# Last weights rebuilt from head 29.5 on, own PSUM tile for a chunk's scale sum, two sets of mixes, later sums of squares

## The chip, the cores and the metric

One NeuronCore of a Trainium2 chip runs the whole program. The metric is the device time of one execution in microseconds, lower is better. TensorE (PE) multiplies matrices into PSUM, VectorE (DVE), ScalarE (ACT) and GpSimd (POOL) do the rest, and SyncE (SP) issues most DMAs. Each engine works through its own list of instructions in order.

## The reference

Three stages, float32 in the result:

```python
# attention: B,H,S,D = 4,8,576,64; decay from cumulated log f, causal softmax
scores = scale * q @ k.T + cum[:, :, :, None] - cum[:, :, None, :]
x = softmax(causal(scores)) @ v                      # -> (4, 576, 512)
# moe: gated MLP, d_model 512, d_ff 1024
h = relu(x @ w_in); u, v = h[..., :512], h[..., 512:]
v_s = einsum('ts,bsd->btd', w_spatial, layernorm(v)) + b_spatial[None, :, None]
x = (u * v_s) @ w_out
# moe2: each token mixed with the one before it
xk = mu_k * x + (1 - mu_k) * x_prev
xr = mu_r * x + (1 - mu_r) * x_prev
k = relu(xk @ w_k)
out = sigmoid(xr @ w_r) * (k * k @ w_v)
```

## The kernel before

Most weights and operands arrive as 64-bit numbers or are kept as a high and a low 16-bit half, so that three matmuls (T3) stand for one product of more exact numbers. A weight block of 128x512 is fetched raw by one DMA of 512 KB (`raw_load`), rebuilt as float32 by one ScalarE and three VectorE instructions (`raw_convert`), squared and summed by ScalarE (`sumsq`), scaled and split into halves (`w2_split`: `scalar.mul`, then a subtraction on VectorE).

The order is written as a list of steps with due times in units of a head (32 heads, `add(t, prio, fn, ...)`); `run` sorts them. The program order that comes out is a priority: a planner of the build places each engine's instructions by a simulated time line, and only instructions given to `pin` keep the program order among themselves. So real places differ from the due times.

- Attention runs head by head. The normalisation of a pair of heads passes through small DMAs on SP (`rd`, `r`, `rd`, `sr`; `head`, `recip`), then GpSimd and ScalarE write `xt`.
- The first MLP of batch b (`plan_mlp`: `m1v` with a layernorm `ln1` to `ln4`, `m1u`, `m2`) follows some heads behind. `m2` (L586) ends with the gate on VectorE (L589), the store of `u` to DRAM and the square of `u` on ScalarE (L594, L66). Batch 3's MLP begins at 34.7 and lasts 4.
- `plan_w2` rebuilds 16 blocks: four of w_out at 13.9 and on, eight of w_k at 25.2 and on, four of w_r at 33.6 and on. The first 12 are fetched through ScalarE's queue, the others by SP. `weights2v` rebuilds the eight blocks of w_v into pool p2, which lies where the MLP's pools `acts` and `w` were.
- The last stage runs over five chunks of up to 512 tokens. `m3(i)` multiplies by w_out, stores `x2[i]` and sums its squares; `mix(i, w)` makes the mixed input `xx[w]` (w = 0 for k, 1 for r), after `scale3`, which adds up the squares with a matmul against ones (`total`, L71, name `tot`) and reduces it on VectorE (L836); `chunk(i)` runs m4 (x w_k, relu, square, split into `k2`), m5 (x w_v, accumulated in four PSUM banks), m6 (x w_r, sigmoid) and multiplies into `o` (L919).
- Pieces of `m3(i+2)` and `mix(i+1, w)` are generators that are advanced between the steps of `chunk(i)`.

PSUM has eight banks here: `psm` tag "m" with two, `ps3` tag "p" with four and tag "a" with two. `total` takes its tile from `psm`, and m5's accumulators 0 and 1 lie in `psm`, 2 and 3 in "a":

```python
ps = self.psm.tile([128, 512], F32, tag="m", name="tot")                       # total, L70
q, tag = (self.psm, "m") if j < 2 else (self.ps3, "a")                         # m5
xh = self.xx[w] = p.tile([128, 2, 4, 512], F16, tag=f"xx{w}", bufs=1, ...)      # mix: one set
```

All matmuls that go through the helper `mm` have line L852 in the profile, whatever the stage; they are told apart by their tiles (`xx,w2k` is m4, `w2r,xx` m6, `moe_w_v,k` m5, `g,wstage` m3; `w2r` holds a part of w_k too, so `xx,w2r` is m4).

Of the kernel before, what the change touches and what calls it, by code (L numbers as in the profile page):

```python
# [39 lines left out]
class K:  # L40
# [19 lines left out]
    def split(self, src, hi, lo):  # L60
        self.nc.scalar.copy(hi, src)
        self.nc.vector.tensor_tensor(lo, src, f32(hi), ALU.subtract)
# [510 lines left out]
    def m2(self, b, fc, hf, part):  # L573
# [13 lines left out]
        if part:  # L587
            uu = self.u[:, fc, ts_]
            nc.vector.scalar_tensor_tensor(uu, o, self.sw[:, 3:4], uu, ALU.mult, ALU.mult)  # L589
            if hf:  # L590
                nc.sync.dma_start(self.gd[:, fc, self.S * b:self.S * b + self.S], self.u[:, fc])
                if fc == 0:
                    self.ga[b] = self.c.tile([128, 4], F32, tag="ga", bufs=2, name="ga")
                self.sumsq(self.ga[b][:, fc:fc + 1], self.u[:, fc], self.junka[:, 0:self.S])  # L594

    def plan_mlp(self, b, s, length):
# [15 lines left out]
        add(s + length + 0.3, 3, self.gsum, b)  # L612
# [89 lines left out]
    def w2_last(self):  # L702
# [4 lines left out]
        self.w2["moe2_w_r"] = [w[:, :, k] for k in range(4)]  # L707

    def w2_fetch(self, n, q):
        nm, kc, c = self.blocks[n]  # L710
        self.raw_load(self.raws[n % 2], nm, slice(128 * kc, 128 * kc + 128), slice(c, c + 512), q)

    def w2_conv(self, n):
# [3 lines left out]
        self.sumsq(self.am2[:, n:n + 1], e, self.junka[:, 0:512])  # L717
# [30 lines left out]
    def plan_w2(self):  # L748

        add = self.add  # L750
        add(13.0, 9, self.w2_begin)
# [8 lines left out]
        add(t[3] + 0.7, 7, self.w2_norm, 0)  # L760
        add(t[11] + 0.7, 7, self.w2_norm, 1)
        add(t[15] + 0.7, 7, self.w2_norm, 2)

    def weights2v(self, p):

        nm = "moe2_w_v"
        self.wv = p.tile([128, 2, 8, 512], F32R, name=nm)
        self.raw_load(self.raws[0], nm, slice(0, 128), slice(0, 512), self.nc.sync)
        yield
        for n in range(8):  # L770
            if n < 7:
                self.raw_load(self.raws[(n + 1) % 2], nm, slice(128 * n + 128, 128 * n + 256), slice(0, 512), self.nc.sync)
            e = self.we[n % 3]
            self.raw_convert(self.raws[n % 2], e, True)
            self.split(e, self.wv[:, 0, n], self.wv[:, 1, n])
            yield
# [10 lines left out]
    def phase3(self):  # L787
# [5 lines left out]
        self.g = [t[:, 2048 + 512 * i:2560 + 512 * i] for i in range(2)]  # L793
# [4 lines left out]
    def m3(self, i):  # L798
# [4 lines left out]
        x2 = self.x2[i] = p.tile([128, 4, 513], F32, tag="x2", bufs=3, name="x2")  # L803
# [14 lines left out]
        for kc in range(4):  # L818
            g, s = self.g[kc % 2], gm[:, 2 + kc:3 + kc]
# [12 lines left out]
    def scale3(self, i):  # L832
# [3 lines left out]
        nc.vector.tensor_reduce(sc[:, 0:1], self.total(self.st3[:, 4 * i:4 * i + 4], 4), AX.X, ALU.add)  # L836
# [17 lines left out]
    def mix(self, i, w):  # L854
# [6 lines left out]
        xh = self.xx[w] = p.tile([128, 2, 4, 512], F16, tag=f"xx{w}", bufs=1, name=f"xx{w}")  # L861
# [16 lines left out]
    def chunk(self, i):  # L878
        nc, p = self.nc, self.p3
        sc = self.sc3[:, 8 * i:8 * i + 8]  # L880
        t0, n = self.chunks[i]
        xk = self.xx[0]
# [4 lines left out]
        def m4(fc):  # L887
            ps = self.ps3.tile([128, 512], F32, tag="p", bufs=4, name="m4")
            self.mm(ps[:, 0:n], [(wk[kc][:, ws, 128 * fc:128 * fc + 128], xk[:, s_, kc, 0:n]) for kc in range(4) for s_, ws in T3])
            tmp = p.tile([128, 512], F32, tag="tmp", bufs=3, name="tmp")  # L890
# [17 lines left out]
        xr = self.xx[1]  # L908
# [16 lines left out]
def body(tc, a, out):  # L925
# [39 lines left out]
    wv = k.weights2v(k.p2)  # L965
    for _ in range(3):
        next(wv, 0)
    for x in first:
# [42 lines left out]
```

## Time and profile before

| | |
|---|---|
| time, median of 3 runs | 775.11 us (771.89 to 775.39) |
| time of the profiled run | 772.58 us |
| its span, first to last instruction | 770.8 us |
| mean granted clock of TensorE | 0.962 of full speed |
| TensorE busy | 675.6 us (88%) |
| VectorE, ScalarE, GpSimd busy | 456.6, 412.9, 191.1 us |
| HBM read, written | 42.06, 9.79 MB |

The profile is one execution. Attention ends at about 395 us, the last MLP's m2 at 490, and the chunks' ends are at 536, 606, 673, 733 and 766 us. Busy time of TensorE is modelled, and matmuls overlap a little. In lists of instructions, the text in square brackets is the time that the engine stood idle before the first of them, and whom it waited for.

### The profile page before, as it was taken

Reading aid. Unit: us, or ns where it says so; the run is one execution under the profiler, and the core shown is the slowest. Engines: PE = TensorE matmul, PEld = TensorE weight load, DVE = VectorE, ACT = ScalarE, POOL = GpSimd, SP = SyncE. Lnnn points to the kernel's source line nnn. Section 1 sums busy time; section 2 is a strip of 40 time slices with the busy share of each in tenths; the row PEclk is TensorE's granted clock in tenths of the full one; section 3 lists DMA queues with packets and bytes.
Section 4 is the critical chain, followed back from the end, with each engine's and each line's share of the span. In section 5 each row is a group of like instructions: output and inputs, shape, how many; then the busy total and the mean of one; then the engine's idle time right before and its main releaser. Section 6 shows DMA issues by size and latency. Waiting matters only on the chain.

```text
span 770.8 us, 11313 instructions
## 1 busy us (share of the span) xinstructions
PE 675.6 (88%) x3742; PEld 429.8 (56%) x3742; DVE 456.6 (59%) x1304; ACT 412.9 (54%) x850; POOL 191.1 (25%) x385
## 2 busy tenths in 40 slices
PE   0388977898989989998899989999899799979988
PEld 0245654566765567655665446566355466636565
DVE  5987794668667646677555883484812462192071
ACT  4636884576546653566665893553832353272251
POOL 7123554454435534444332300000000000000000
PEclk9998979999999999999999999999999899999999
DMA  9997867665663424432144311251000100010010
GB/s 228 201 202 159 184 131 155 139 148 115 159 161 102 100 53 76 90 107 70 58 140 144 110 27 45 70 154 57 25 14 1 55 1 1 1 55 0 1 56 27
DMA packets 130683, 69.80 MB, mean 91 GB/s; under 512 B 114704, under 2 KB 115312, under 8 KB 130624
## 3 DMA queue, kind: packets, MB, share of 16 engines
q1 hardware_dynamic: 126304, 61.59, 33.5%
q10 hardware_dynamic: 4320, 7.48, 3.4%
q8 instruction: 29, 0.48, 0.3%
q14 instruction: 30, 0.25, 0.1%
HBM read 42.06 MB, written 9.79 MB: 67 GB/s over the span
## 4 chain that ended last, share of the span: by engine, by line
PE 52%; DMA 16%; DVE 13%; ACT 7%; POOL 5%; issue 4%; SPq 3%; ACTq 0%; DVEq 0%; POOLq 0%
PE m L852 35%; PE o L370 5%; PE m L586 4%; DMA sr<-rd 3%; POOL x L401 3%; DMA rd<-xo 3%; DMA r<-rd 2%; PE m1u L569 2%; PE s L315 2%; DVE junk L324 2%; PE t L348 2%; DMA nat<-in_k_dram 2%; DVE o L919 2%; DMA rd<-r 2%; ACT junka L66 1%
## 5 line engine op out<-in xcount | busy, mean ns | idle before, releaser
L370 PE MATMUL o<-e,v 128*128 128x320 f32 (+4 forms) x448 | 118.0, 395 | 13.6 <-ACT xo L378 7.0
L852 PE MATMUL m<-moe_w_v,k 128*128 128x512 f32 x432 | 110.8, 407 | 0.0
L852 PE MATMUL m<-xx,w2k 128*128 128x512 f16 (+1 forms) x360 | 84.4, 377 | 17.0 <-ACT xx L874 17.0
L370 PEld LDWEIGHTS o<-e,v 128*128 128x128 f32 x448 | 79.8, 204 | 32.7 <-POOL e L357 9.2
L324 DVE CUSTOM_DVE_ANT_0 junk<-s,mask 128x512 bf16<-128x512 f32 (+4 forms) x160 | 75.7, 473 | 28.8 <-PE s L315 23.6
L852 PEld LDWEIGHTS m<-moe_w_v,k 128*128 128x128 f32 x432 | 80.8, 188 | 20.6
L352 ACT ACTIVATE e<-t,qa 128x512 f32<-128x512 f32 (+1 forms) x128 | 71.6, 590 | 33.6 <-PE t L348 31.4
L357 POOL TENSOR_SCALAR_AFFINE_SELECT e<-e 128x128 f32<-128x128 f32 (+1 forms) x160 | 53.2, 351 | 118.3 <-ACT e L352 115.8
L315 PE MATMUL s<-kT,qT 128*128 128x512 f16 (+2 forms) x192 | 55.5, 300 | 24.1 <-DVE nm L324 14.7
L852 PEld LDWEIGHTS <-w2k 128*128 128x128 f16 x360 | 36.2, 103 | 53.5 <-issue 25.0
L893 DVE TENSOR_TENSOR tmp<-tmp 128x512 f32<-128x512 f32 (+1 forms) x40 | 25.1, 638 | 65.7 <-ACT tmp L892 65.5
L401 POOL TENSOR_TENSOR x<-xo,sr 64x576 f32<-64x576 f32 x32 | 47.4, 1481 | 64.5 <-DMA sr<-rd 63.2
L569 PE MATMUL m1u<-xt,win 128*128 128x288 f16 x384 | 55.1, 294 | 5.8 <-ACT u L571 3.5
L348 PE MATMUL t<-qA,kA 69*128 69x512 f16 (+2 forms) x192 | 50.9, 292 | 7.6 <-DMA qA<-md 4.9
L515 PE MATMUL m1v<-win,xt 128*128 128x512 f16 x240 | 57.2, 379 | 0.0
L315 PE MATMUL s<-kA,qA 67*128 67x512 f16 (+2 forms) x192 | 50.6, 302 | 5.3 <-DMA kA<-kT 3.4
L852 PE MATMUL m<-g,wstage 128*128 128x512 f16 (+1 forms) x240 | 54.8, 375 | 0.0
L892 ACT ACTIVATE tmp<-m,w2k 128x512 f32<-128x512 f32 (+1 forms) x40 | 25.1, 644 | 55.0 <-PE m L852 54.9
L586 PE MATMUL m<-wspT,vn 128*128 128x288 f16 x384 | 53.5, 286 | 0.4 <-DVE u L589 0.4
L348 PE MATMUL t<-qT,kT 128*128 128x512 f16 (+2 forms) x192 | 50.2, 292 | 0.0
L569 PEld LDWEIGHTS <-win 128*128 128x128 f16 x384 | 38.3, 101 | 19.7 <-issue 7.4
L852 PE MATMUL m<-w2r,xx 128*128 128x512 f16 x216 | 48.2, 379 | 0.0
(206 smaller groups left out, 1144.1 us busy)
## 6 DMA issues: line engine op xcount, KB each, us to landing
sr<-rd SPq DMA_DIRECT2D x32, 144.0 KB
gd<-u SPq DMA_DIRECT2D x16, 288.0 KB
out_dram<-o SPq DMA_DIRECT2D x18, 256.0 KB
nat<-in_k_dram SPq DMA_DIRECT2D x32, 128.0 KB
v<-in_v_dram SPq DMA_DIRECT2D x32, 128.0 KB
wstage<-in_moe_w_k_dram ACTq DMA_DIRECT2D x8, 512.0 KB
g<-gd SPq DMA_DIRECT2D x16, 256.0 KB
wstage<-in_moe_w_v_dram SPq DMA_DIRECT2D x8, 512.0 KB
```

What stands on the lines that cost most here:

```text
L315: self.nc.tensor.matmul(s[:, o:o + n], self.tok(qn, p, h, 128 * ib - 64, 128)[0:r], self.tok(kn, p, h, k0, n)[0:r], start=(j == 0), stop=( ...
L324: self.nc.vector.tensor_tensor_reduce(out=self.junk[r0:, 0:n], in0=self.s[u % 2][r0:, o:o + n], in1=self.mask[r0:, m0:m0 + n], op0=ALU.add ...
L348: self.nc.tensor.matmul(t[:, o:o + n], self.tok(kn, p, h, 128 * c, 128)[0:r], self.tok(qn, p, h, q0, n)[0:r], start=(j == 0), stop=(j == 1))
L352: self.nc.scalar.activation(self.e[g][:, 512 * u:512 * u + n], t[:, 0:n], AF.Exp, scale=self.qa[p][:, 5:6])
L357: self.nc.gpsimd.affine_select(out=e, in_=e, pattern=[[1, n]], compare_op=ALU.is_ge, fill=0.0, base=0, channel_multiplier=-1)
L370: self.nc.tensor.matmul(o[:, 256 + f:256 + q1], v[:, c, h // 2, 64 * (h % 2):64 * (h % 2) + 128], e[:, off:off + q1 - f], start=(c == 0), ...
L401: self.nc.gpsimd.tensor_tensor(self.xp[r], self.xo[h][r], self.sr[r], ALU.mult)
L515: nc.tensor.matmul(self.m1p, xt[:, xs, 128 * j:128 * j + 128], self.win[:, ws, kc, 512:1024], start=(kc == 0 and n == 0), stop=(kc == 3 an ...
L569: self.nc.tensor.matmul(o, self.win[:, ws, kc, fs], self.xt[(4 * b + kc) % 8][:, xs, ts_], start=(kc == 0 and n == 0), stop=(kc == 3 and n ...
L586: nc.tensor.matmul(o, pairs[n][0], pairs[n][1], start=(n == 0), stop=(n == 13))
L852: self.nc.tensor.matmul(out, l, r, start=(first and j == 0), stop=(last and j == len(pairs) - 1))
L892: nc.scalar.activation(tmp[:, 0:n], ps[:, 0:n], AF.Relu, scale=sc[:, 4:5])
```

## The change

- `total` can take its tile from another pool; `scale3` passes `ps3`, so the chunk's scale sum lies in the ring "p", of four tiles.
- `xx` has two sets: even chunks in p3, odd ones in p2. `k2`, `o` move from p3 to p2; w_v moves from p2 to p3; `x2` has two buffers in place of three; the staging tiles `g` of m3 are three in place of two.
- All 16 blocks of `plan_w2` come from 29.5 on, 0.33 apart, and w_v's eight blocks behind them, 0.36 apart, as steps of the list. All fetches are issued by SP.
- The squares of the weight blocks and of `u` become steps of their own, some tenths of a head later, and are pinned; so is the ScalarE half of w_v's split.
- Before the chunks, `m3(0), m3(1), mix(0, 0), mix(0, 1)` are advanced from the first of the remaining steps on, and all done before the pools are released. In the chunk loop the side work is advanced at each step.

```diff
-    def total(self, col, n):
-        ps = self.psm.tile([128, 512], F32, tag="m", name="tot")
+    def total(self, col, n, p=None):
+        ps = p.tile([128, 512], F32, tag="p", bufs=4, name="tot") if p else self.psm.tile([128, 512], F32, tag="m", name="tot")
...
@@ m2
                 nc.sync.dma_start(self.gd[:, fc, self.S * b:self.S * b + self.S], self.u[:, fc])
-                if fc == 0:
-                    self.ga[b] = self.c.tile([128, 4], F32, tag="ga", bufs=2, name="ga")
-                self.sumsq(self.ga[b][:, fc:fc + 1], self.u[:, fc], self.junka[:, 0:self.S])
@@ plan_mlp
-        add(s + length + 0.3, 3, self.gsum, b)
+            if k == "g" and x[1] and x[2]:
+                add(t + (0.5 if b < 3 else 0.2), 3, self.gsq, b, x[0])
+        add(s + length + (0.7 if b < 3 else 0.3), 3, self.gsum, b)
+    def gsq(self, b, fc):
+        if fc == 0:
+            self.ga[b] = self.c.tile([128, 4], F32, tag="ga", bufs=2, name="ga")
+        self.pin(self.sumsq(self.ga[b][:, fc:fc + 1], self.u[:, fc], self.junka[:, 0:self.S]))
@@ w2_fetch, w2_conv
-        self.raw_load(self.raws[n % 2], nm, slice(128 * kc, 128 * kc + 128), slice(c, c + 512), q)
+        self.raw_load(self.raws[n % 2], nm, slice(128 * kc, 128 * kc + 128), slice(c, c + 512), self.nc.sync)
-        self.sumsq(self.am2[:, n:n + 1], e, self.junka[:, 0:512])
+    def w2_sq(self, n):
+        self.pin(self.sumsq(self.am2[:, n:n + 1], self.e2[n], self.junka[:, 0:512]))
@@ plan_w2
-        t = [13.9 + 1.5 * i for i in range(4)] + [25.2 + 1.0 * i for i in range(8)] + [33.6 + 0.45 * i for i in range(4)]
+        t = [29.5 + 0.33 * i for i in range(16)]
         for n in range(16):
-            add(13.1 if n == 0 else max(24.6 if n == 4 else 0, t[n] - 0.9), 9, self.w2_fetch, n, self.nc.scalar if n < 12 else self.nc.sync)
+            add(29.0 if n < 2 else t[n - 1] + 0.02, 9, self.w2_fetch, n)
             add(t[n], 7, self.w2_conv, n)
             if not 4 <= n < 12 or n % 2:
-                add(t[n] + 0.35, 7, self.w2_split, n)
+                add(t[n] + 0.3, 7, self.w2_split, n)
+            add(t[n] + 0.25, 7, self.w2_sq, n)
...
+        tv = [t[15] + 0.36 * (i + 1) for i in range(8)]
         for n in range(8):
+            add(t[15] + 0.02 if n == 0 else tv[n - 1] + 0.02, 9, self.wv_fetch, n)
+            add(tv[n], 7, self.wv_conv, n)
+            add(tv[n] + 0.25, 7, self.wv_split, n)
@@ phase3, m3
-        self.g = [t[:, 2048 + 512 * i:2560 + 512 * i] for i in range(2)]
+        self.g = [t[:, 2048 + 512 * i:2560 + 512 * i] for i in range(2)] + [self.g2]
-        x2 = self.x2[i] = p.tile([128, 4, 513], F32, tag="x2", bufs=3, name="x2")
+        x2 = self.x2[i] = p.tile([128, 4, 513], F32, tag="x2", bufs=2, name="x2")
@@ scale3, mix, chunk
-        nc.vector.tensor_reduce(sc[:, 0:1], self.total(self.st3[:, 4 * i:4 * i + 4], 4), AX.X, ALU.add)
+        nc.vector.tensor_reduce(sc[:, 0:1], self.total(self.st3[:, 4 * i:4 * i + 4], 4, self.ps3), AX.X, ALU.add)
-        xh = self.xx[w] = p.tile([128, 2, 4, 512], F16, tag=f"xx{w}", bufs=1, name=f"xx{w}")
+        xh = self.xx[i, w] = (self.p2 if i % 2 else p).tile([128, 2, 4, 512], F16, tag=f"xx{w}", bufs=1, name=f"xx{w}")
-        nc, p = self.nc, self.p3
+        nc, p = self.nc, self.p2
@@ body
-    first = (x for y in (k.m3(0), k.mix(0, 0), k.m3(1)) for x in y)
+    first = (x for y in (k.m3(0), k.m3(1), k.mix(0, 0), k.mix(0, 1)) for x in y)
     while k.steps:
         last += 0.25
         k.run(last)
-        if last > G + 2.0:
-            next(first, 0)
+        next(first, 0)
+    for _ in first:
+        pass
...
         for _ in k.chunk(i):
-            next(wv, 0)
-            n += 1
-            if (n <= 5 and i < 3) or n >= 9:
-                next(side, 0)
-            if n == 12:
-                next(side, 0)
+            next(side, 0)
```

## Rows read from the trace of the kernel before

**Rows 1.** Page, engines' busy time, share of the span, instructions.

```profile
PE 675.6 (88%) x3742; PEld 429.8 (56%) x3742; DVE 456.6 (59%) x1304; ACT 412.9 (54%) x850; POOL 191.1 (25%) x385
```

**Rows 2.** Waits of PE from 520 on: us in total, times, longest.

```profile
PE m L852 <- ACT xx L874: 17.0, 4, 4.7
```

**Rows 3.** Timeline of PE around the second boundary: start, us, what.

```profile
608.51 0.28 PE L71 MATMUL tot<-w2k,ones 128*128 128x4 f32 x2
613.45 1.86 PE L852 MATMUL m<-xx,w2k 128*128 128x512 f16 x4 [4.66 <-ACT xx L874]
```

**Rows 4.** Chain of waits over the second boundary: start, us, what.

```profile
606.67 0.66 DVE o L919
...
609.45 0.09 DVE w2k L836
...
610.71 1.96 ACT tmp L871 x3
```

**Rows 5.** Windows behind the boundaries, and the middle of a chunk; PEclk is granted clock.

```profile
core 0: us, PE busy (x) PEld busy (x) DVE busy (x) ACT busy (x) POOL busy (x), PEclk, DMA share, GB/s
543.00:547.00 4.00, 4.00 (x11) 1.46 (x11) 4.00 (x9) 3.73 (x6) 0.00 (x0) 0.57 0.00 0
613.45:617.50 4.05, 4.05 (x16) 2.21 (x16) 4.05 (x10) 3.58 (x6) 0.00 (x0) 0.50 0.00 0
679.50:683.50 4.00, 4.00 (x11) 1.46 (x11) 4.00 (x9) 3.68 (x6) 0.00 (x0) 0.57 0.00 0
738.50:741.00 2.50, 2.48 (x12) 1.72 (x12) 2.50 (x8) 2.50 (x8) 0.00 (x0) 0.50 0.00 0
620.00:672.00 52.00, 52.00 (x254) 31.76 (x252) 14.15 (x23) 17.71 (x33) 0.00 (x0) 1.00 0.00 1
```

**Rows 6.** Windows of the last MLP and the first chunk.

```profile
440.00:450.00 10.00, 4.88 (x34) 3.23 (x33) 8.82 (x26) 9.76 (x24) 2.66 (x11) 1.00 0.20 52
450.00:460.00 10.00, 9.94 (x54) 5.57 (x54) 7.37 (x12) 8.86 (x18) 0.00 (x0) 0.83 0.00 0
400.00:490.00 90.00, 84.44 (x508) 50.10 (x507) 55.33 (x130) 55.95 (x122) 13.14 (x30) 0.98 0.28 88
490.00:536.00 46.00, 46.00 (x209) 27.56 (x207) 28.36 (x61) 26.51 (x47) 0.19 (x1) 1.00 0.30 93
```

**Rows 7.** Single lines of a weight block: ns min/median/max, first and last start.

```profile
L105 ACT ACTIVATE wstage<-wstage x26: 642/662/689, 12.2 to 523.8; 128x512 f32<-128x512 f32 x26
L61 ACT CAST moe_w_v<-wstage x6: 609/619/622, 498.6 to 526.5; 128x512 fp32r<-128x512 f32 x6
L108 DVE TENSOR_SCALAR wstage<-wstage x32: 406/423/1473, 16.7 to 524.1; 128x512 int32<-128x512 int32 x32
L112 DVE SCALAR_TENSOR_TENSOR wstage<-wstage x26: 671/688/1793, 19.0 to 524.6; 128x512 int32<-128x512 int32 x26
L113 DVE SCALAR_TENSOR_TENSOR wstage<-wstage x26: 670/691/1565, 19.7 to 525.8; 128x512 int32<-128x512 int32 x26
L62 DVE TENSOR_TENSOR moe_w_v<-wstage,moe_w_v x6: 679/692/706, 499.2 to 527.2; 128x512 fp32r<-128x512 f32 x6
```

**Rows 8.** Groups of PE from 443 to 490 by form: busy, mean, idle before.

```profile
L852 PE MATMUL m<-xx,w2k 128*128 128x512 f16 x36 | 10.6, 406 | 0.0
L852 PE MATMUL m<-xx,w2r 128*128 128x512 f16 x12 | 3.7, 379 | 0.0
```

**Rows 9.** Waits of ACT and of PE over the whole span.

```profile
ACT junka L66 <- DVE u L589: 15.5, 6, 4.8
...
PE o L370 <- ACT xo L378: 7.0, 5, 3.5
```

**Rows 10.** Waits of SP; an issue on ScalarE's queue; transfers of the chain.

```profile
SPq L98 <- DVE wstage L113: 16.8, 6, 7.6
...
378.20 0.33 ACTq L98 DMA_DIRECT2D wstage<-in_moe_w_k_dram  x1
...
355.27 1.57 DMA r<-rd
378.35 3.38 DMA r<-rd
```

More of the change, by code (lines that the diff above doesn't have):

```diff
@@ L58, in pin, with split @@
         self.tc.keep_in_program_order(ins)
-    def split(self, src, hi, lo):
-        self.nc.scalar.copy(hi, src)
+    def split(self, src, hi, lo, pin=False):
+        x = self.nc.scalar.copy(hi, src)
+        if pin:
+            self.pin(x)
         self.nc.vector.tensor_tensor(lo, src, f32(hi), ALU.subtract)
@@ L707, in w2_last, with w2_fetch @@
         self.w2["moe2_w_r"] = [w[:, :, k] for k in range(4)]
[L709 removed]
+        self.g2 = t[:, 3072:3584]
+    def w2_fetch(self, n):
         nm, kc, c = self.blocks[n]
[L711 removed]
+        self.raw_load(self.raws[n % 2], nm, slice(128 * kc, 128 * kc + 128), slice(c, c + 512), self.nc.sync)
     def w2_conv(self, n):
@@ L750, in plan_w2, with wv_fetch, wv_conv, wv_split @@
         add = self.add
-        add(13.0, 9, self.w2_begin)
+        add(24.4, 9, self.w2_begin)
         add(24.45, 9, self.w2_more)
         add(26.3, 9, self.w2_last)
-        t = [13.9 + 1.5 * i for i in range(4)] + [25.2 + 1.0 * i for i in range(8)] + [33.6 + 0.45 * i for i in range(4)]
+        t = [29.5 + 0.33 * i for i in range(16)]
         for n in range(16):
-            add(13.1 if n == 0 else max(24.6 if n == 4 else 0, t[n] - 0.9), 9, self.w2_fetch, n, self.nc.scalar if n < 12 else self.nc.sync)
+            add(29.0 if n < 2 else t[n - 1] + 0.02, 9, self.w2_fetch, n)
             add(t[n], 7, self.w2_conv, n)
             if not 4 <= n < 12 or n % 2:
-                add(t[n] + 0.35, 7, self.w2_split, n)
[L760 to L769, printed above, removed]
-        for n in range(8):
[L771 to L776, printed above, removed]
+                add(t[n] + 0.3, 7, self.w2_split, n)
+            add(t[n] + 0.25, 7, self.w2_sq, n)
+        for x, n in enumerate((3, 11, 15)):
+            add(t[n] + 0.4, 7, self.w2_norm, x)
+        tv = [t[15] + 0.36 * (i + 1) for i in range(8)]
+        for n in range(8):
+            add(t[15] + 0.02 if n == 0 else tv[n - 1] + 0.02, 9, self.wv_fetch, n)
+            add(tv[n], 7, self.wv_conv, n)
+            add(tv[n] + 0.25, 7, self.wv_split, n)
+    def wv_fetch(self, n):
+        self.raw_load(self.raws[n % 2], "moe2_w_v", slice(128 * n, 128 * n + 128), slice(0, 512), self.nc.sync)
+    def wv_conv(self, n):
+        if n == 0:
+            self.wv = self.p3.tile([128, 2, 8, 512], F32R, name="moe2_w_v")
+        e = self.we[(n + 1) % 3]
+        self.raw_convert(self.raws[n % 2], e, True)
+        self.e2[n] = e
+    def wv_split(self, n):
+        self.split(self.e2.pop(n), self.wv[:, 0, n], self.wv[:, 1, n], True)
     def runs(self, t0, n):
@@ L818, in m3 @@
         for kc in range(4):
-            g, s = self.g[kc % 2], gm[:, 2 + kc:3 + kc]
+            g, s = self.g[(4 * i + kc) % 3], gm[:, 2 + kc:3 + kc]
             nc.sync.dma_start(g[:, 0:n], self.gd[:, kc, t0:t0 + n])
@@ L889, in m4 @@
             self.mm(ps[:, 0:n], [(wk[kc][:, ws, 128 * fc:128 * fc + 128], xk[:, s_, kc, 0:n]) for kc in range(4) for s_, ws in T3])
-            tmp = p.tile([128, 512], F32, tag="tmp", bufs=3, name="tmp")
+            tmp = self.p3.tile([128, 512], F32, tag="tmp", bufs=3, name="tmp")
             t = k2[fc] = p.tile([128, 2, 512], F32R, tag="k2", bufs=4, name="k2")
@@ L907, in chunk @@
             yield
-        xr = self.xx[1]
+        xr = self.xx[i, 1]
         for j in range(J):
@@ L964, in body @@
     k.p2 = k.pool("phase2", side="left")
-    wv = k.weights2v(k.p2)
-    for _ in range(3):
-        next(wv, 0)
-    for x in first:
-        next(wv, 0)
-    for x in k.mix(0, 1):
-        next(wv, 0)
     for i in range(5):
@@ L974, in body @@
         side = (x for y in ys for x in y)
-        n = 0
         for _ in k.chunk(i):
-            next(wv, 0)
-            n += 1
-            if (n <= 5 and i < 3) or n >= 9:
-                next(side, 0)
-            if n == 12:
-                next(side, 0)
+            next(side, 0)
         for _ in side:
-            next(wv, 0)
+            pass
     for p in (k.ps3, k.psm, k.p2, k.p3, k.kp, k.hl, k.ar, k.c):
```

2 lines of the change are left out of this document (1 added, 1 removed).

## The prediction, made before the changed kernel ran

> **What bounds the kernel now.** Read the page first: TensorE is busy 88% of the span [rows 1], so a change is worth what it does to TensorE's idle time and clock. Next the list of waits of TensorE in the last stretch, from 520 us on: one wait stands in it, four times, 17.0 us together [rows 2]. The timeline shows where: the last m5 matmul of a chunk, then one small matmul named tot, then nothing for 4.66 us until the first m4 of the next chunk, which waited for xx, the chunk's mixed input [rows 3]. The chain of waits names the cause: VectorE multiplies the accumulators into o from 606.67, only then reduces tot at 609.45, then ScalarE begins the mix at 610.71 [rows 4]. Tot is the chunk's scale sum. It takes a PSUM tile "m" of the pool psm, which has two, and both hold m5 accumulators until o has been multiplied. So the mix, which needs nothing of this chunk, can't start before the chunk is over. All four boundaries look alike. TensorE's clock is at 1.2 instead of 2.4 GHz after each gap: granted 0.57, 0.50, 0.57 and 0.50 in the four stretches behind, 1.00 in the middle of a chunk [rows 5].
>
> Then the stretch before, by tens of microseconds. Between 440 and 460 TensorE is idle 5.2 us while ScalarE is busy 18.6 of 20 (last batch's MLP, first mixes); over 400 to 490 VectorE is busy 55.3 and ScalarE 56.0 of 90; from 490 to 536 TensorE never stops [rows 6].
>
> **Part 1: own tile for the sum, two sets of mixes, tiles moved.** total() gets a tile from ps3's ring "p" of four, so it can run while the accumulators are held; xx of odd chunks lies in p2, so mix(i+1) may write while chunk i still reads its own set. In chunk i the side work is m3(i+2), then both mixes of i+1: 5+4+4 = 13 steps against 14 steps of the chunk, so it fits. Gain: the four gaps, 17.0, and the half-speed stretches behind them. The loss there is (1 − granted) times length: 0.43 x 4.00 + 0.50 x 4.05 + 0.43 x 4.00 + 0.50 x 2.50 = 6.7 us [rows 5]. Sum 23.7 us. What hides the mix now: in 620 to 672 VectorE is busy 14.2 and ScalarE 17.7 of 52 [rows 5], and a mix adds eight passes of some 0.7 us on each per set. Cost 0; if that cover were gone, the gap of 4.66 would be back. The sum's tile occupies one of the four "p" slots for a few instructions: 0, since slots turn over while m5 runs in between; at worst the start of one m4, and nothing below 0. x2 with two buffers is free: m3(i+2) overwrites x2[i], whose mixes are now done a chunk earlier. What is late next at a boundary: m5 of the new chunk needs the accumulators freed, and it comes only after three m4, while the four multiplications take 2.8 us (from 606.67 to 609.45) [rows 4]. Nothing.
>
> **Part 2: the weights.** 12 of the 16 blocks (w_out, w_k) leave positions 13.9 to 32.2; all 16 stand at 29.5 to 34.45 and w_v's eight blocks at 34.8 to 37.3. A w_v block costs ScalarE 0.66+0.62 = 1.28 us and VectorE 0.42+0.69+0.69+0.69 = 2.49 [rows 7]; a w2 block has the same steps plus a square on ScalarE, which I take at a pass of 0.62, and small scalars, so some 1.9 and 2.5. Eight w_v blocks: ScalarE 10.2, VectorE 19.9. Today they lie behind 490, where TensorE doesn't stop, so removing them there brings nothing; they go into 400 to 490, as do some four w2 blocks (half of the ones now done before 395, by position). New load of these 90 us: VectorE 55.3+19.9+10.0 = 85.2, ScalarE 56.0+10.2+7.6 = 73.8. It fits in sum, but VectorE almost fills the stretch and ScalarE was the limit at 440 to 460. Bounds of the cost: 0 (everything finds a hole, w_v itself isn't wanted before m5) and 14.3 us, the m4 matmuls that today fill TensorE in 443 to 490 (10.6+3.7) [rows 8] and would find no input in time. Below 0 is possible only by the idle 5.2 us. I take 5, nearer to the low end since TensorE's 5.2 us idle stand at the same ScalarE load.
>
> k2 and o move to p2, on memory that the last MLP frees. Today two or three m4 results are handled before 490; tmp has three buffers and "p" four, so that many m4 can wait without k2. Cost 0, and 14.3 without that cover, the same bound [rows 8].
>
> Before 395, seven or more blocks disappear from ScalarE and VectorE, and the squares of u are issued later and held there: they made ScalarE idle 15.5 us in six waits, and TensorE waited 7.0 us for xo, which stands in the same queue [rows 9]. Behind a held square stand the exponentials and xo copies of the next heads; later, the square finds its data there. Bounds of the gain: 0 and 7.0. I take 2, since the single stall of 3.5 that makes half of the 7.0 stands behind a cast that waits for GpSimd, which stays. New pins can also cost: a square that is pinned holds every later pinned conversion. That is in the range.
>
> **Queues.** Twelve fetches move from ScalarE's queue to SP's, where w_r's and w_v's already are. SP stands still in a fetch that waits for its buffer: 16.8 us in six waits, longest 7.6 [rows 10]. Behind it stand rd, r and sr of the last pairs (the normalisation that the last MLP reads) and g of m3. ScalarE is freed of 0.33 us per issue. A small transfer beside a fetch of 512 KB on the other queue took 3.38 us against 1.57 without one [rows 10]. Cost taken 0, inside the 5 above; its bad case is the last rival.
>
> The Trainium skill (DMA: Bandwidth & Descriptors, Queues, rings and completion order) says that a DMA engine takes turns, packet by packet, between the queues that have work for it. By that rule the fetch on ScalarE's queue should let the small one through, and on SP's own queue the small one stands behind all of it, which speaks against the move. The trace bears out only half: even on separate queues the small one lost 1.8 us. By the rule the loss is larger than 1.8 per transfer; the sum above would be some 5 us higher if each of the last pair's four transfers lost 1.3 more (an estimate).
>
> **Sum.** The profiled run took 772.58, 2.5 below the median of three and inside their spread: 772.58 − 23.7 + 5 − 2 = 751.9, say 752. Runs of the new kernel may lie up to 3 above it in the same way.
>
> **Rivals.**
> A, starved end of the MLP. The gaps go, but the weights fill ScalarE and VectorE in 400 to 490 and TensorE loses all the fill: 772.6 − 23.7 + 14.3 = 763, to 766 with half-speed stretches behind new gaps. For it: VectorE at 85 of 90. Against: lists are placed by a planner that puts blocks into holes, and TensorE's order can be changed.
> B, the gaps halve only. The tile is no longer the hold, but the mix is placed late, behind m3's work, or g's transfers stand behind output transfers on SP. Half of 23.7 stays: 772.6 − 11.9 + 3 = 764. Against: 13 steps in 14, and engines more than half idle.
> C, it doesn't do what it says: the sum's matmul is still placed behind m5, as it needs a "p" slot; all gaps stay, and the stretch costs 0 to 5: 770 to 778, take 774.
> D, slower. SP as one line for all: a fetch waits for its raw buffer, that waits for VectorE's conversion, and the last two pairs' rd, r, sr wait behind. With the longest wait of 7.6 at each of the last pair's four steps, 30.4, and 1.8 more for each landing, 7.2, the last MLP starts 37.6 later: 772.6 − 23.7 + 37.6 = 786. It is slower than now from 23.7 us of delay on, that is three such full waits. Against: the mean of the six is 2.8, which gives 11 us.
> E, better: the stretch costs 0, the waits for xo all go: 772.6 − 23.7 − 7 = 742.
>
> **How the numbers follow.** Forecast (743 to 760) 0.58, A 0.15, B 0.08, C 0.05, D 0.06, E 0.08. Range 741 to 766: forecast, E mostly, A and B, about 0.84 before what I may have missed. 0.5% of the median is 3.9 us, about what a measurement can tell from no change. Faster than 771.2: forecast, A, B, E, less a little: 0.87. Same: most of C and the tails: 0.07. Slower: D and a bit of C: 0.06.
>
> **What would show it.** Right: no wait of TensorE for xx of several us from 520 on, tot of chunk i+1 amid chunk i, granted clock 1.00 across the boundaries, w_v converted before the first m5. A shows as idle TensorE between 400 and 500 with VectorE or ScalarE as releaser; B and C as gaps at the boundaries; D as long SP waits of fetches ahead of rd, r, sr. The forecast is wrong if the planner reorders the heads before 395 so that attention changes by more than 5 us: no row before speaks for the size of that.

## The result, and the profile of the changed kernel

The changed kernel takes 765.19 us (median of 7 runs, 764.05 to 769.39), the kernel before, run beside it, 775.11 (770.78 to 777.08): ratio 0.9895, 95% interval 0.9861 to 0.9929. It is faster by 1.05%, where 752, 3% less, was forecast. The time lies inside the range (741 to 766), at its very end, where rival A stood.

The page first (engines' busy time with its share of the span; then the span of 763.4 us in 40 slices, each digit the busy tenths of TensorE and its granted clock):

```profile
PE 670.8 (88%) x3742; PEld 428.2 (56%) x3742; DVE 452.3 (59%) x1304; ACT 413.8 (54%) x850; POOL 184.0 (24%) x385
...
PE   0378978989989999999789826999999999999998
...
PEclk9998979989998999999999977999999999999999
```

Next to [rows 1] the engines do the same work: TensorE 4.8 us less, VectorE 4.3 less. From slice 25 on (counted from 0) TensorE reads 9, in the clock too, but for the end of the last slice. The holes are ahead of that: slices 19 and 20 and, above all, 23 and 24 (19.1 us a slice, so some 439 to 477), with a clock of 7.

The waits of TensorE from 380 to the end (engine and line, what it waited for: us in total, times, longest):

```profile
PE m L865 <- ACT xx L887: 9.4, 1, 9.4
PE tot L73 <- ACT junka L68: 7.2, 1, 7.2
PE o L372 <- POOL e L359: 4.0, 1, 4.0
PE tot L73 <- ACT junka L754: 3.5, 1, 3.5
PE m1v L517 <- ACT vt L525: 2.5, 1, 2.5
```

The wait of [rows 2] for xx, 17.0 us in four, is gone as a group: all five lie ahead of 470, and from 556 on not one wait of TensorE is listed. What a boundary looks like now, in TensorE's timeline around the first one (start, us, what); it answers [rows 3]:

```profile
529.04 0.28 PE L73 MATMUL tot<-w2k,ones 128*128 128x4 f32 x2
529.18 2.10 PE L865 MATMUL m<-xx,w2k 128*128 128x512 f16 x9
...
550.14 5.94 PE L865 MATMUL m<-moe_w_v,k 128*128 128x512 f32 x24
555.93 1.25 PE L865 MATMUL m<-xx,w2k 128*128 128x512 f16 x5
```

Tot of chunk 1 runs in the middle of chunk 0, 21 us ahead of the last run of m5, and the first m4 of chunk 1 follows that m5 with no idle time in brackets. So the diagnosis of the boundary and its cure were right.

Now the whole span by stages: attention, from the last heads and batch MLPs to the end of chunk 0, and chunks 1 to 4. The cuts are at the same points of the work in both kernels. Columns: stretch, its length, busy time of PE, PEld, DVE, ACT, POOL (instructions), granted clock, DMA share, GB/s. First the kernel before, then the changed one, whose last line is the hole.

```profile
40.00:395.60 355.60, 318.58 (x1963) 214.30 (x1962) 241.07 (x801) 212.66 (x457) 158.60 (x309) 0.95 0.54 120
395.60:538.50 142.90, 137.34 (x758) 82.64 (x757) 89.67 (x217) 85.93 (x176) 13.33 (x31) 0.99 0.30 94
538.50:770.80 232.30, 211.48 (x992) 127.84 (x991) 96.21 (x212) 92.67 (x170) 0.19 (x1) 0.96 0.06 21
```

```profile
40.00:383.40 343.40, 311.53 (x1916) 209.81 (x1916) 216.09 (x749) 198.96 (x424) 150.97 (x308) 0.95 0.53 115
383.40:556.10 172.70, 147.49 (x804) 88.72 (x803) 123.08 (x303) 110.18 (x225) 16.50 (x32) 0.93 0.31 97
556.10:763.40 207.30, 203.55 (x990) 124.64 (x988) 84.37 (x178) 83.19 (x154) 0.19 (x1) 1.00 0.06 23
...
440.00:460.00 20.00, 3.93 (x19) 1.93 (x18) 16.33 (x46) 14.56 (x36) 5.30 (x15) 0.73 0.27 88
```

- Chunks 1 to 4: 232.30 to 207.30, 25.0 us less. TensorE's idle time falls from 20.8 to 3.75 and its busy time from 211.5 to 203.6, with the clock from 0.96 to 1.00.
- Attention: 12.2 us less. 7.05 of it is TensorE work (318.58 to 311.53; 47 matmuls fewer here, 46 more in the middle) that only moved behind the cut; its idle time falls from 37.0 to 31.9, by 5.1.
- The middle: 29.8 us more. Idle 5.6 to 25.2; busy 10.2 more, 7 of it the work that moved in; the other 3 go with the lower clock (0.93 for 0.99). Without the moved work it lost 22.8.

In total 25.0 + 12.2 − 29.8 = 7.4 us, the difference of the two profiled spans. With the moved work taken out of both sides, three quarters of the gains (22.8 of 30.1) were given back. Most of the middle's 25.2 us of idle time lies in one place: three waits of some 19 us in all between 440 and 463. In 440 to 460 TensorE works 3.93 of 20 us (14.83 in the kernel before), with VectorE busy 16.3.

What TensorE does there, from its timeline (brackets: idle time before, and what ended it):

```profile
443.12 2.75 PE L517 MATMUL m1v<-win,xt 128*128 128x512 f16 x12 [2.53 <-ACT vt L525]
453.12 0.59 PE L73 MATMUL tot<-w2k,ones 128*128 128x4 f32 x2 [7.25 <-ACT junka L68]
463.07 3.87 PE L865 MATMUL m<-xx,w2k 128*128 128x512 f16 x10 [9.37 <-ACT xx L887]
466.78 0.28 PE L73 MATMUL tot<-nn,ones 128*128 128x1 f32 x2
466.92 0.36 PE L73 MATMUL tot<-ga,ones 128*128 128x4 f32 x2
...
468.86 1.39 PE L571 MATMUL m1u<-xt,win 128*128 128x288 f16 x10
```

The scale sum of chunk 0 waits in the in-order list, then chunk 0's first m4. Two more small sums and the last batch's m1u, which runs without a wait at 468.86, stand behind them. The square that the scale sum waits for is late in ScalarE's own list, between steps of weight blocks and of the MLP: the last part of x is written at 434.93, its last square comes at 452.35.

```profile
434.93 0.68 ACT L840 ACTIVATE x<-m,g 128x512 f32<-128x512 f32 x1
...
452.35 0.63 ACT L68 ACTIVATE junka<-x 128x512 bf16<-128x512 f32 x1
```

And what VectorE does between that scale sum and the mix:

```profile
453.74 0.16 DVE L849 TENSOR_REDUCE w2k<-tot 128x1 f32<-128x4 f32 x1 [0.36 <-PE tot L73]
453.82 0.74 DVE L743 SCALAR_TENSOR_TENSOR w2r<-wstage,rs,w2r 128x512 f16<-128x512 f32 x1
454.48 0.42 DVE L110 TENSOR_SCALAR wstage<-wstage 128x512 int32<-128x512 int32 x1
...
454.94 0.69 DVE L114 SCALAR_TENSOR_TENSOR w2k<-w2k,wstage 128x512 int32<-128x512 int32 x1
...
456.72 0.68 DVE L115 SCALAR_TENSOR_TENSOR w2k<-wstage,w2k 128x512 int32<-128x512 int32 x1
...
458.46 0.22 DVE L860 TENSOR_SCALAR w2k<-w2k 128x8 f32<-128x8 f32 x1
```

From the reduction of tot to the mix's coefficients it takes 4.7 us (453.74 to 458.46), since the steps of weight blocks (L110, L114, L115, L743) and of the last batch's v lie between the small steps of some 0.15. At the first boundary the same chain, to the same line, runs from 529.36 to 530.39, 1.0 us.

How the blocks came, read from ScalarE's first step of a block: before, the 16th starts at 433.03. In the changed kernel the first starts at 360.13 and the 16th at 451.23, 6.1 us apart on average. They are due 0.33 of a head apart, some 3.5 us (so the first five come in the run with less of VectorE's work, below: 359.52, 363.50, 367.34, 370.66, 373.57).

VectorE wasn't full in that time. It was busy 63.3 of the 91.2 us from the first block to the 16th (and 25.1 of the first 40, where the blocks already come 4.8 to 8.8 us apart, but for one):

```profile
360.00:451.23 91.23, 71.72 (x409) 42.50 (x407) 63.33 (x164) 60.44 (x131) 21.59 (x40) 0.95 0.42 131
```

The way of one block, from its first step on ScalarE to that of the next, 5.9 us here, shows what takes the time:

```profile
364.97 0.66 ACT L107 ACTIVATE wstage<-wstage 128x512 f32<-128x512 f32 x1
...
367.02 0.69 DVE L115 SCALAR_TENSOR_TENSOR wstage<-wstage 128x512 int32<-128x512 int32 x1
368.30 0.62 ACT L68 ACTIVATE junka<-wstage 128x512 bf16<-128x512 f32 x1
369.04 0.15 DVE L80 TENSOR_SCALAR rs<-wstage 128x1 f32<-128x1 f32 x1 [1.33 <-ACT junka L68]
...
370.28 0.71 ACT L742 ACTIVATE wstage<-wstage,rs 128x512 f16<-128x512 f32 x1
370.89 0.66 ACT L107 ACTIVATE wstage<-wstage 128x512 f32<-128x512 f32 x1
```

ScalarE begins the block, VectorE merges it, ScalarE squares it, VectorE makes the scale, ScalarE applies it, and each waits for the other. In ScalarE's list the next block's first step stands directly behind the scaling or the square of the block before in 14 of the 15 cases. So the blocks pass one at a time, and the length of this chain is their pace.

### The profile page after: what moved, and what is told of

It reads as the page before. It is cut to its first block, busy times and chain, and to the rows that moved or that the text cites. A ratio compares the mean times of both kernels' runs of the same rounds, so it can differ in the third digit from the quotient of the medians.

```text
span 763.4 us, 11316 instructions
## 1 busy us (share of the span) xinstructions
PE 670.8 (88%) x3742; PEld 428.2 (56%) x3742; DVE 452.3 (59%) x1304; ACT 413.8 (54%) x850; POOL 184.0 (24%) x385
## 4 chain that ended last, share of the span: by engine, by line
PE 62%; DMA 12%; DVE 10%; ACT 6%; POOL 5%; issue 3%; SPq 2%; ACTq 0%; DVEq 0%; POOLq 0%
PE m L865 35%; PE o L372 7%; PE m L588 6%; PE t L350 4%; PE m1u L571 3%; PE s L317 3%; PE m1v L517 3%; DMA sr<-rd 2%; POOL x L403 2%; DVE junk L326 1%; ACT junka L68 1%; DMA wstage<-in_moe_w_k_dram 1%; DMA qA<-md 1%; DMA md<-mr 1%; DMA rd<-r 1%
## 5 line engine op out<-in xcount | busy, mean ns | idle before, releaser
L865 PE MATMUL m<-xx,w2k 128*128 128x512 f16 (+1 forms) x360 | 79.4, 363 | 9.4 <-ACT xx L887 9.4
L905 ACT ACTIVATE tmp<-m,w2k 128x512 f32<-128x512 f32 (+1 forms) x40 | 25.7, 644 | 74.2 <-PE m L865 74.1
L517 PE MATMUL m1v<-win,xt 128*128 128x512 f16 x240 | 60.5, 399 | 3.3 <-ACT vt L525 2.5
L865 PEld LDWEIGHTS <-w2k 128*128 128x128 f16 x360 | 34.4, 100 | 44.3 <-issue 16.3
L571 PE MATMUL m1u<-xt,win 128*128 128x288 f16 x384 | 52.9, 286 | 1.0 <-ACT u L573 1.0
L865 PE MATMUL m<-g,wstage 128*128 128x512 f16 (+1 forms) x240 | 50.8, 358 | 0.1
L588 PEld LDWEIGHTS <-vn 128*128 128x128 f16 x384 | 37.7, 100 | 13.6 <-issue 2.3
```

The costliest lines, as they stand in the source:

```text
L517: nc.tensor.matmul(self.m1p, xt[:, xs, 128 * j:128 * j + 128], self.win[:, ws, kc, 512:1024], start=(kc == 0 and n == 0), stop=(kc == 3 an ...
L571: self.nc.tensor.matmul(o, self.win[:, ws, kc, fs], self.xt[(4 * b + kc) % 8][:, xs, ts_], start=(kc == 0 and n == 0), stop=(kc == 3 and n ...
L588: nc.tensor.matmul(o, pairs[n][0], pairs[n][1], start=(n == 0), stop=(n == 13))
L865: self.nc.tensor.matmul(out, l, r, start=(first and j == 0), stop=(last and j == len(pairs) - 1))
L905: nc.scalar.activation(tmp[:, 0:n], ps[:, 0:n], AF.Relu, scale=sc[:, 4:5])
```

## The experiments

The questions: is it the due times of the weight blocks that cost the middle (and not the new tile, the squares, the queue or the other order of the first chunk's work)? If so, what paces the blocks, and why does TensorE stand? In each pair of numbers "ratio" is to the kernel before, run beside it, with its 95% interval. The first four ran on one chip together (kernel before 773.5 us), the next four (772.9), the next three (773.1), and the last alone (771.5).

**The first part alone**: the kernel before with tot in its own tile, two sets of mixes, and one side step at each step of a chunk.

```diff
...
+        ps = p.tile([128, 512], F32, tag="p", bufs=4, name="tot") if p else self.psm.tile([128, 512], F32, tag="m", name="tot")
...
+        nc.vector.tensor_reduce(sc[:, 0:1], self.total(self.st3[:, 4 * i:4 * i + 4], 4, self.ps3), AX.X, ALU.add)
...
+        xh = self.xx[i, w] = (self.p2 if i % 2 else p).tile([128, 2, 4, 512], F16, tag=f"xx{w}", bufs=1, name=f"xx{w}")
...
-            if (n <= 5 and i < 3) or n >= 9:
-                next(side, 0)
-            if n == 12:
-                next(side, 0)
+            next(side, 0)
```

> The kernel before with Part 1 alone: the scale sum in the ring p, two sets of mixes, side work advanced at each chunk step; weights, squares and queues as before. Theory 1 (Part 1 is worth what its gaps were, and the stretch from 383 to 556 us lost it through the moved weights): the gaps at the chunk boundaries go, the stretch stays as before, time 748 to 753. Rival (the boundaries close only because w_v and the mixes were moved early, and w_v's rebuild beside chunk 0 now collides with the mixes): gaps remain at the first boundary, time above 758.

Measured: 751.39 us, ratio 0.9725 (0.9697 to 0.9754), 22.2 us less. Faster than the whole change by 14. Of the waits of TensorE from 380 on these are over a microsecond:

```profile
PE tot L71 <- ACT junka L66: 3.5, 1, 3.5
PE m1v L515 <- ACT vt L523: 3.3, 1, 3.3
```

None is at a boundary: both lie ahead of 460. The first part does what was worked out for it, and the rest of the change takes time.

**The squares of u back where they were**, in m2 and not held, all else of the change kept.

```diff
+                self.gsq(b, fc)
...
-            if k == "g" and x[1] and x[2]:
-                add(t + (0.5 if b < 3 else 0.2), 3, self.gsq, b, x[0])
...
-        self.pin(self.sumsq(self.ga[b][:, fc:fc + 1], self.u[:, fc], self.junka[:, 0:self.S]))
+        self.sumsq(self.ga[b][:, fc:fc + 1], self.u[:, fc], self.junka[:, 0:self.S])
```

> The changed kernel with the squares of u again inside m2, unpinned and undelayed. Theory 2 (the held squares keep the single buffer u of batch 2 until 461.8 us, so m1u of batch 3 can't be stored, and TensorE has nothing ready): the stretch shortens by at least half of its 23 us, time 750 to 756. Theory 1 (load and order of the weights in the stretch): time within 4 of the changed kernel, 762 to 770, and the 5 us gained in attention may go back.

Measured: 762.27, ratio 0.9871 (0.9841 to 0.9901), against 0.9895 (0.9861 to 0.9929) with the squares held. The intervals overlap, and the time is where the theory of the weights had it (762 to 770); TensorE still waits 8.7 us for xx and 6.9 and 4.0 for two tot. The held squares are no more than a small part of it.

**The old due times**: the change with its 16 blocks where they were. (W_v's blocks, due behind the last of them, come 0.5 of a head later.)

```diff
-        add(24.4, 9, self.w2_begin)
+        add(13.0, 9, self.w2_begin)
...
-        t = [29.5 + 0.33 * i for i in range(16)]
+        t = [13.9 + 1.5 * i for i in range(4)] + [25.2 + 1.0 * i for i in range(8)] + [33.6 + 0.45 * i for i in range(4)]
...
```

> The changed kernel with the due times of the 16 blocks as before (13.9, 25.2, 33.6 and on); queue, squares, w_v's steps and Part 1 as changed. Theory 1: the blocks are what delays the stretch, most of the 23 us come back, time 745 to 753. Theory 2 (held u): the squares are still pinned and late, at most half comes back, 756 to 764.

Measured: 747.6 us, ratio 0.9651 (0.9595 to 0.9707): 17.6 less than the change, and faster than both kernels. TensorE's waits from 380 on:

```profile
PE tot L73 <- ACT junka L754: 1.9, 1, 1.9
PE m1u L571 <- DVE nn L80: 1.1, 1, 1.1
```

No other is over 0.5. The holes went with the due times alone. The 16th block starts at 429.63.

**w_v later**: its eight blocks due from 38.9 of a head on.

```diff
-        tv = [t[15] + 0.36 * (i + 1) for i in range(8)]
+        tv = [38.9 + 0.2 * (i + 1) for i in range(8)]
...
```

> The changed kernel with w_v's eight blocks behind the last MLP (due 38.9 on, 0.2 apart), all else as changed. If w_v's 20 us of VectorE in the stretch are the load that matters: the idle time of TensorE in 430 to 475 shrinks by half, time 752 to 758. If the 16 blocks or the held squares matter, w_v comes after the damage: time 761 to 770, TensorE's idle time between 430 and 463 stays.

Measured: 765.65, ratio 0.9905 (0.9868 to 0.9943), the same as the change; TensorE is busy 4.80 of the 20 us from 440. So it isn't w_v, the only weight that the prediction had priced whole.

**The small matmuls after the last batch's m1u**, by due times: norms of w_k and w_r from 37.25, the first mixes from 5.4 after the heads' end.

```diff
-            add(t[n] + 0.4, 7, self.w2_norm, x)
+            add(max(t[n] + 0.4, 37.25 if x else 0), 7, self.w2_norm, x)
...
-        next(first, 0)
+        n0 += 1
+        if n0 <= 10 or last > G + 5.4:
+            next(first, 0)
```

> The changed kernel with the norms of w_k and w_r (a tot matmul each) due at 37.25, behind the last m1u, and the first two mixes started there too; blocks, squares, queues as changed. Theory 1b (TensorE's list: tot matmuls that wait for late weights stand ahead of MLP work that is ready): the waits for tot and xx between 430 and 463, some 20 us, are filled by m2, m1v and m1u; time 748 to 756. Theory 1a (the pace of the blocks delays all that needs them; whatever is put ahead, m4 comes late): TensorE's idle time moves behind the MLP, time 761 to 768.

Measured: 767.28, ratio 0.9923 (0.9891 to 0.9955). It didn't do what it was meant to. TensorE's timeline:

```profile
452.40 0.59 PE L73 MATMUL tot<-w2k,ones 128*128 128x4 f32 x2 [15.58 <-ACT junka L68]
459.04 0.59 PE L73 MATMUL tot<-ga,ones 128*128 128x4 f32 x2 [6.05 <-ACT junka L68]
459.49 2.80 PE L571 MATMUL m1u<-xt,win 128*128 128x288 f16 x11
```

The scale sum and batch 2's sum, which waits for a held square, still stood ahead of m1u; 21.6 us of waiting went into these two. It says where the list stands, not what it costs.

**Earlier blocks**: the same 16 in a row, from 25.0 with 0.63 between.

```diff
-        t = [29.5 + 0.33 * i for i in range(16)]
+        t = [25.0 + 0.63 * i for i in range(16)]
...
```

> The changed kernel with the 16 blocks spread from 25.0 to 34.45 (0.63 apart) in place of 29.5 to 34.45 (0.33 apart): same last due time, an earlier start. Theory 1a (at 0.33 head, 3.6 us, the blocks can't keep their due times; they came 5.7 to 6.2 us apart and some 25 us late): with 0.63 head, 6.8 us, they keep them, most of the loss comes back, time 746 to 753. If late blocks aren't the cause: 761 or more.

Measured: 754.26, ratio 0.9753 (0.972 to 0.9787), 11 less than the change. The 16th block starts at 426.94, 2.7 ahead of the old due times, and TensorE is busy 16.73 of the 20 us from 440. The old times themselves are 6.7 better still, so the start of the last block isn't the whole cost. The traces don't show where the 6.7 lies: the two profiled executions are only 1.3 apart (749.86 and 748.59).

**No fetches**: blocks 2 to 15 are rebuilt from what lies in the raw buffers; their transfers are left out.

```diff
-            add(29.0 if n < 2 else t[n - 1] + 0.02, 9, self.w2_fetch, n)
+            if n < 2:
+                add(29.0, 9, self.w2_fetch, n)
```

> The changed kernel without the fetches of blocks 2 to 15, which are rebuilt from what lies in the two raw buffers; the output is not the reference's. If the pace of the blocks is set by the two raw buffers (a fetch may start only when the block two before is rebuilt, then lands 4.9 us later): blocks come 3.6 to 4.5 us apart, time 746 to 755. If it is set by the engines' work itself: still 5.5 us or more apart, time 760 or more.

Measured: 764.21, ratio 0.9886 (0.9848 to 0.9924). Nothing is gained: the 16th block starts at 452.92, and the blocks keep their pace. The transfers, and the wait of each for a raw buffer, don't pace them.

**Twelve fetches on ScalarE's queue**, as in the kernel before, all else of the change kept.

```diff
-        self.raw_load(self.raws[n % 2], nm, slice(128 * kc, 128 * kc + 128), slice(c, c + 512), self.nc.sync)
+        self.raw_load(self.raws[n % 2], nm, slice(128 * kc, 128 * kc + 128), slice(c, c + 512), self.nc.scalar if n < 12 else self.nc.sync)
```

> The changed kernel with the fetches of blocks 0 to 11 on ScalarE's queue again. If SP's line holds back the stretch (42 us of waits for a raw buffer with rd, r, sr and the stores behind them): 3 us or more faster, 757 to 762. If the queue doesn't matter: within 2 us, 763 to 767.

Measured: 774.46, ratio 1.002 (0.9995 to 1.0045): 9.3 slower than the change, where the expectations were 3 or more faster, or no difference. The 16th block starts at 458.90, 7.7 later. The move of the queue, costed at nothing, is worth nearly all of the 9.9 us that the whole change gained.

**The list of TensorE, written out**: four small matmuls (two norms, batch 2's sum, chunk 0's scale sum) held behind the last batch's m1u; batch 2's squares back in m2, and the due times of the run with the small matmuls after m1u.

```diff
+        x = self.nc.tensor.matmul(ps[:, 0:n], self.ones, col, start=True, stop=True)
+        if pin:
+            self.pin(x)
...
+                if b == 3:
+                    self.pin(x)
...
```

> In a_tot_behind_u two tot matmuls still stood ahead of m1u: the scale sum of the first mix and the sum of u's squares of batch 2, whose last square came at 458. Here all four tot matmuls that wait for late work (two norms, that sum, the first scale sum) are pinned behind batch 3's m1u on TensorE, and batch 2's squares are issued inside m2, not held; blocks as changed. Theory 1b (TensorE's list): m1u fills the hole, TensorE's idle time between 430 and 470 falls from 20 to under 8 us, and with it the time: 749 to 756. Theory 1a (the pace of the blocks): the hole is filled, but m4 and the end of the MLP come as late, the idle time shows up behind it; 761 to 768.

Measured: 758.34, ratio 0.9813 (0.9791 to 0.9836), 6.9 less than the change and between the two expectations (749 to 756, 761 to 768). TensorE's longest waits from 380 on:

```profile
PE m1u L573 <- ACT u L577: 9.8, 1, 9.8
PE o L374 <- POOL e L361: 3.6, 1, 3.6
PE m L873 <- ACT xx L895: 2.5, 1, 2.5
```

The waits for tot and most of that for xx are gone, and 9.8 us of waiting have come back at m1u itself, whose results ScalarE takes out too late. The order of the list, with batch 2's squares, is worth some 7 of the 17.6 us; the rest needs earlier blocks.

**Less of VectorE**: its two merging steps (L114, L115) are left out for the 16 blocks.

```diff
...
+        if not merge:
+            return
         nc.vector.scalar_tensor_tensor(ei, ei, 3, low, ALU.logical_shift_left, ALU.bitwise_or)
         nc.vector.scalar_tensor_tensor(ei, high, -2147483648, ei, ALU.bitwise_and, ALU.bitwise_or)
...
```

> The changed kernel with the two merging steps of VectorE (0.69 us each) left out for the 16 blocks; the output is not the reference's. Some 22 us of VectorE's work less in 360 to 460. If VectorE's work sets the pace of the blocks: they come 4.5 us apart or less, block 15 before 435 instead of 451, time 748 to 756. If the pace is set elsewhere (the planner's places, ScalarE): blocks still 5.5 us or more apart, time 760 or more.

Measured: 742.07, ratio 0.9606 (0.9572 to 0.9641), 23 less than the change and 6 better than the better expectation. The due times are the late ones, and the 16th block starts at 425.42. The windows of the former hole:

```profile
440.00:460.00 20.00, 18.41 (x115) 11.59 (x114) 18.01 (x42) 17.30 (x36) 6.00 (x5) 0.94 0.32 95
460.00:480.00 20.00, 20.00 (x129) 12.48 (x128) 15.70 (x28) 11.05 (x21) 0.59 (x1) 1.00 0.22 70
```

TensorE is busy 38.4 of 40. What was taken away is 16 x (0.69 + 0.69) = 22 us of VectorE, by the durations of [rows 7]; it brings the last block 25.8 us forward, with the blocks 4.4 us apart. So VectorE's two steps lie on the way that paces the blocks. The run takes load off VectorE and shortens each block's chain in one, and can't tell the two apart; that VectorE was busy 63.3 of 91.2 us in the changed kernel speaks for the chain.

**Late blocks alone**: the kernel before with nothing but its 16 blocks at the new due times, fetched through SyncE's queue.

```diff
...
-        t = [13.9 + 1.5 * i for i in range(4)] + [25.2 + 1.0 * i for i in range(8)] + [33.6 + 0.45 * i for i in range(4)]
+        t = [29.5 + 0.33 * i for i in range(16)]
...
```

> The kernel before with the 16 blocks alone at the changed due times (29.5 on, 0.33 apart, fetched by SP); all else as before, gaps at the boundaries too. If the late blocks cost by themselves: 15 to 20 us slower than before, 788 to 794. If they cost only beside the other parts of the change (w_v's steps, held squares): within 6 of before, 770 to 780.

Measured: 790.72, ratio 1.0228 (1.0201 to 1.0256), 17.6 more than the kernel before. TensorE's waits from 380 on:

```profile
PE m L851 <- ACT xx L873: 16.8, 4, 4.4
PE tot L71 <- ACT junka L745: 13.3, 2, 7.7
PE tot L71 <- ACT junka L66: 4.7, 2, 2.6
```

The four gaps of [rows 2] are untouched, and 18.0 us of waits for two kinds of tot are added. The late blocks cost the same with the boundaries mended or not, so the terms add: the prediction had the right form of sum.

**Old due times on ScalarE's queue**, to price the queue where nothing is late.

```diff
-        self.raw_load(self.raws[n % 2], nm, slice(128 * kc, 128 * kc + 128), slice(c, c + 512), self.nc.sync)
+        self.raw_load(self.raws[n % 2], nm, slice(128 * kc, 128 * kc + 128), slice(c, c + 512), self.nc.scalar if n < 12 else self.nc.sync)
...
-        t = [29.5 + 0.33 * i for i in range(16)]
+        t = [13.9 + 1.5 * i for i in range(4)] + [25.2 + 1.0 * i for i in range(8)] + [33.6 + 0.45 * i for i in range(4)]
...
```

> The changed kernel with its 16 last blocks at the old due times (as in the run at the old times, 747.6 us) and, beside that, the fetches of the first 12 of them issued by ScalarE again instead of SyncE. Theory that the queue matters wherever ScalarE is busy with the blocks: slower than 747.6 by about as much as at the late times, 755 to 758. Theory that the queue mattered only because the blocks had become late: within 3 us of 747.6, like the kernel before with the tile and the sets alone (751.4), which also fetches on ScalarE's queue. If the queue is worth nothing at the old times, the blocks' first steps stand within 3 us of those at the old times with SyncE's queue.

Measured: 752.03, ratio 0.9755 (0.9711 to 0.9799), against 0.9651 (0.9595 to 0.9707) with SyncE's queue. That lies between the two expectations: 4.4 us by the medians, 8 by the ratios, with intervals that all but touch; the two ran on different occasions. It is the time of the first part alone (751.39), which fetches on the same queue. The 16th block starts 4.4 later than with SyncE's queue (434.06 for 429.63). So the move gains something at the old times too, and how much isn't settled.

## Why the prediction was right in direction and wrong in size

**What bounds the kernel, and Part 1: right.** Forecast −23.7; the chunks' stretch lost 25.0, and the first part alone is 22.2 faster. Each sign named for it is there: no wait for xx at a boundary, tot amid the chunk before, clock 1.00. That the side work fits, that the sum's slot of the ring costs nothing, and that m5 isn't late next all held: from 556 on no wait is listed. B and C fell with that.

**Part 2: the step that failed.** It took 5 us, with 14.3 as the worst. The trace gives 22.8 for the middle, the runs 17.6 (the change against the old due times; late blocks alone). Two parts of the step were wrong:

- "It fits in sum." The sum did fit: VectorE was busy 74.1 of the 90 us from 400 to 490, where the prediction had put it at 85.2. But a load that fits says nothing of when its last result is ready. Each block is a chain that passes between ScalarE and VectorE, and the next block's first step stands behind it in ScalarE's list. Blocks due 3.5 us apart came 6.1 apart, the last of the 16 started 18 us later than before (451.23 for 433.03), and the run whose chains lack VectorE's two merging steps brought it back to 425.42 and the time to 742. The prediction put the delay at what TensorE would lack meanwhile, and never worked out when the last block would be ready.
- The bound. 14.3 was the m4 work that fills the stretch today [rows 8], as if the worst were to lose the fill. But TensorE's list is in order, and at its head stood matmuls that end a long chain over ScalarE and VectorE: tot waited 7.25 us for a square, whose data were written 17 us before its turn in ScalarE's list, m4 waited 9.37 for the mix, and the last batch's m1u stood behind. What stood still was also work that was not fill at all. Holding four of these behind m1u gave 6.9 us back; the remaining 11 came back with earlier blocks.

Both are in the prediction as words: VectorE "almost fills the stretch" spoke for A, and against A stood that "TensorE's order can be changed". The choice "nearer to the low end since TensorE's 5.2 us idle stand at the same ScalarE load" read a load where a chain over both engines set the pace.

**Rival A** gives the right time, 763 to 766, and its sign, idle TensorE in 400 to 500 with ScalarE behind VectorE as releaser, is what the trace shows. Its working is right in part only: the middle lost more than its 14.3, and attention gave 5 back, so that its time came out right is partly luck. So is it that the time fell inside the range: with the twelve fetches on ScalarE's queue, whose move was put at 0, it would have been 774.

**Attention: −2, bounds 0 and −7.** TensorE's idle time ahead of 383 fell by 5.1, inside the bounds. Of this, the waits for xo fell from 7.0 to 3.0. They stay low with the squares back in m2 (2.2) and are high again with the blocks at their old times (5.8), so it is the blocks that left, not the held squares. The single wait of 3.5, which the prediction took to stay, is gone with them (longest 0.8). The rest of the 5.1 wasn't taken apart.

**Queues: cost 0, and the sign was wrong.** Moving twelve fetches to SyncE's queue gains 9.3 us at the late times and 4 to 8 at the old. D's sign is there, but not what it should lead to: SyncE waits in fetches for VectorE, far longer than the 16.8 us in six waits of [rows 10] (which leave out 8.2 more in four, for fetches into w2k). The waits of SyncE's queue in the changed kernel, from 380 to 500 alone:

```profile
SPq L100 <- DVE wstage L115: 42.3, 11, 8.3
...
SPq L100 <- DVE w2k L115: 15.6, 5, 7.9
```

57.9 us in sixteen waits. They don't price the move, nor do they cost much by themselves: in the same window SyncE waits 55.7 us with the twelve fetches on ScalarE's queue, and 56.6 in the fast kernel at the old due times. What the queue does to the blocks: with the twelve fetches on ScalarE's queue the first block starts 3.2 us later than in the change, the sixth 2.7, the seventh 7.2, the last 7.7. What stands ahead of the seventh, in ScalarE's list:

```profile
402.32 0.67 ACT L406 CAST xt<-x 128x576 f16<-128x576 f32 x1 [5.04 <-POOL x L403]
...
404.14 0.66 ACT L107 ACTIVATE w2k<-wstage 128x512 f32<-128x512 f32 x1
```

That xt belongs to the last pair of heads, and GpSimd had waited for its small transfer sr, which took 6.35 us (394.38 to 400.73). In the change sr of the last pair lands in at most 3.8 us, and the seventh block (396.97) stands ahead of xt (398.54). So a good part of the delay arises at the last pair's transfer and in the order of ScalarE's list, which changed along with the queue. This is read from one trace of each kernel, and no run took the two apart: the mechanism is argued, not shown.

The Trainium skill (DMA: Bandwidth & Descriptors, Queues, rings and completion order) says that a DMA engine turns from queue to queue by packets; the prediction drew from it that small transfers would lose on SyncE's queue. No run here shows that loss: the kernels with the fetches on SyncE's queue are the faster ones in both comparisons, and the slow sr (6.35 us) is in the kernel with its fetches on ScalarE's queue.

**The sum again, with what was measured**: 772.6 − 25.0 (chunks) − 5.1 (attention) + 22.8 (the middle) = 765.3, the profiled run (765.16) to 0.1. The stretches are cut without a rest, so it has to come out and proves nothing by itself; the gain of the queue is inside these terms.

The best version that ran with the whole computation is the change at the old due times, 747.6 us: the two gains without the loss.

## What to carry to other kernels

When a change moves a block of work into a stretch, don't ask only whether it fits in that stretch's busy time: follow one piece of it through the in-order lists of its engines, up to the step that the next piece stands behind. That length, times the pieces, says when the last result is ready; then look who stands behind that in TensorE's list. Here the cost, 17.6 us, was near the delay of that result (18 us against the kernel before, 22 against the old due times) and not near the work that the stretch would lack. And price a moved due time by a run of its own: here one line of due times held back 18 of the 25 us that the rest of the change had won.

## What was not expected

- The queue that issues a fetch was worth 9.3 us here (774.46 against 765.19) though every transfer, its size and its due time were the same, and leaving fourteen of the transfers out altogether was worth nothing (764.21).
- The chain of small VectorE steps from a scale sum to its coefficients takes 1.0 us where VectorE has room (529.36 to 530.39) and 4.7 where weight blocks share its list (453.74 to 458.46). It isn't the length alone that hurts: at the old due times it runs from 447.93 to 453.58, longer still, and TensorE has other work queued ahead there.
